# Moving the low halves of three weight tensors by 384 bytes in on-chip memory

## The chip, the cores and the metric

The kernel runs on one core of a Trainium2 chip. It is timed as one program: the metric is the device time of one execution in microseconds (us), and the number that stands for the kernel is the median of several executions. Beside the timed executions there is one that the hardware profiler recorded; all rows of views in this document come from such a recorded execution. Engines are named as the profile names them: PE is the matrix engine (TensorE), PEld its loading of weights, DVE is VectorE, ACT is ScalarE, POOL is GpSimd, SP is SyncE, which issues the DMAs.

## The reference

An attention layer with product features feeds a gated feed-forward layer with a mixing step along the sequence. Cut to what matters:

```python
# 4 batches, 4 heads, 1088 positions, head width 32; model width 128, hidden 1024
def phi(x):                                   # 8 x 8 products of two small projections
    a = np.einsum('rd,bhsd->bhsr', S1, x)
    b = np.einsum('rd,bhsd->bhsr', S2, x)
    return np.einsum('bhsi,bhsj->bhsij', a, b).reshape(*x.shape[:-1], 64)
kv  = np.einsum('bhsf,bhsd->bhfd', phi(k), v)
num = np.einsum('bhsf,bhfd->bhsd', phi(q), kv)
den = np.einsum('bhsf,bhf->bhs', phi(q), phi(k).sum(2))[..., None] + 1e-06
x   = (num / den) with heads joined           # 4 x 1088 x 128
h   = np.maximum(x @ w_in, 0.0)
u, v = h[..., :512], h[..., 512:]
v_n = (v - mean(v)) / sqrt(var(v) + 1e-06)    # over the 512 columns
v_s = np.einsum('ts,bsd->btd', w_spatial, v_n) + b_spatial[None, :, None]
out = (u * v_s) @ w_out
```

The step with `w_spatial` (1088 x 1088, applied to 512 columns of each of four batches) is most of the arithmetic.

## The kernel before

**Three products for one.** Every large matmul is split into a high and a low part of each operand, in a rounded four-byte format (float32r), and made of three matmuls: high by high, high by low, low by high. `mm3` (lines 424 to 427) does it for the dense layers. For the spatial step, `high` issues `vh` by `wTh` (line 943) and `vl` by `wTh` (line 945), and `low` issues `vh` by `wTl` (line 952); the last, half-filled block of 64 rows is done with the extra tile `v9` (line 954). In all of these the first-named operand, `vh` or `vl`, is the stationary one: PE loads it as 128 x 128 weights (a row LDWEIGHTS of PEld with the same line) while the matmul before still streams its own moving operand.

**Tiling.** A batch has 1088 output positions, cut into three column blocks of 424, 332 and 332 (`CH`), and 512 hidden columns, cut into four groups `d` of 128. One block (d, c) of the spatial step runs over nine steps `kt` along the contracted positions; each step is three matmuls in the order 943, 945, 952, and the last step is 943, 954. So a block streams 26 matmuls into one bank of PSUM (`sp`). Around the blocks stand the groups of three matmuls for `u` (tile `pu`, weights `wih0` and `wil0`, moving operand `x`), for the output layer (tile `po`, weights `woh` and `wol`, moving operand `g` or `x`), and for the next batch's attention and hidden layer (tile `sd`). The first batch is different: its first column block runs `kt` by `kt` over all four d as the data arrive, with lines 943 and 945 alone in turn, and the line 952 follows after it.

**Who writes the low parts.** `vl` is written by DVE (line 892 in the first batch, line 863 later), `wil0` and `wol` once at the start by DVE (line 435), each as the full value less its rounded high part. No DMA reads or writes them.

**What sets the order.** A planner in the kernel (`Order`) has a list of all operations with their costs and due times, orders them for all engines before the program is built, and the instructions are emitted in that order. Addresses play no part in it.

**Where tiles lie.** Most tiles of on-chip memory (SBUF) get their home when first used. The large weights have theirs at the head of `tile_kernel`, in a fixed sequence (lines 377 to 386), each right behind the one before in every partition. In the built program this gives, in bytes from the start of a partition and modulo 256:

| tiles | address | modulo 256 |
|---|---|---|
| `vh`, `wih0`, `woh` | 1632, 20064, 22112 | 96, 96, 96 |
| `ka1` (384 bytes) | 24160 | 96 |
| `vl`, `wil0`, `wol` | 24544, 40928, 42976 | 224, 224, 224 |
| `wT`, columns of block 0 / 1 / 2 | from 45088 | 32 / 240 / 240 |
| `x`, columns of block 0 / 1 / 2 | from 133408 | 32 / 192 / 240 |
| `g`, 424-wide / 332-wide pieces | from 128032 | 32 / 240 |
| `v9` (the last step's weights) | 158688 | 224 |

One step of `kt` is 2048 bytes in `vh` and `vl` and 4608 bytes in `wT`, one d is 512 bytes, so every weight that PE loads from a tile has the remainder that stands in the table.

Of the kernel before, what the change touches and what calls it, by code (L numbers as in the profile page):

```python
# [356 lines left out]
def tile_kernel(ctx: ExitStack, tc: tile.TileContext, kT, qT, vA, sks, idn, msk, wT, w_in, w_out, bsp, out):  # L357
# [12 lines left out]
    def weights(*names):  # L370
        for x in names:
            if x in ("vh", "vl"):
                homes[x] = const.tile([P, NS if x == "vh" else NK, ND, P], F32R, name=x)
            else:
                fixed[x] = const.tile([P, DH], F32R, name=x)

    homes["ka", 0] = const.tile([P, 96], F32, name="ka0")
    fixed["b32"], fixed["mask_sb"] = const.tile([P, 16], F32, name="b32"), const.tile([P, 6], F32, name="mask_sb")
    weights("vh", "wih0", "woh")
    homes["ka", 1] = const.tile([P, 96], F32, name="ka1")  # L380
    weights("vl", "wil0", "wol")
    homes["rec", 0] = const.tile([P, 3 * H], F32, name="rec0")
    homes["wT"] = const.tile([P, 2 * NS * PITCH], F32R, name="wT")
    homes["g"] = const.tile([P, SB_BUFS["g"], G_PITCH], F32R, name="g")
# [143 lines left out]
    wol = tl(None, "wol", [P, ND, DM], F32R)  # L528
# [583 lines left out]
```

## Time and profile before

| | |
|---|---|
| median of 3 executions | 331.39 us (331.07 to 331.58) |
| the profiled execution, its own time | 331.01 us |
| its span, first to last instruction | 329.2 us |
| PE busy | 323.0 us, 98% of the span, 2308 matmul records |
| PEld busy | 311.2 us, 95% |
| DVE, ACT, POOL busy | 200.3, 158.0, 59.4 us |
| granted PE clock | 1.0 throughout |

So 1.8 us of the profiled execution's time lie outside the span. A row of a timeline has the start and the length of an instruction; matmuls are pipelined, their lengths are modelled and overlap, so the pace of PE is read from the distance between two starts and not from the lengths. A row of groups has line, engine, operation, output and inputs, sizes, count, busy time and mean length of one.

### The profile page before, as it was taken

The page shows a single profiled execution, that of the slowest core. Times are in us where ns is not written, and L with a number is a line of the kernel's source. Part 1 is how long each engine was busy: PE and PEld are TensorE (multiplying, and loading weights), DVE is VectorE, ACT ScalarE, POOL GpSimd, SP SyncE. Part 2 cuts the span into 40 slices and gives each one's busy share as a digit, 9 for nine tenths or more (in the row PEclk, how much of TensorE's full clock was granted, in tenths as well). Part 3 has the DMA queues.
Part 4 walks back from the last instruction along what each step waited for, and adds up shares of the span by engine and source line. Part 5 has one row for each costly group of instructions (what it writes and reads, how often), then busy time and mean ns, then how long its engine had stood idle before and what let it go on. Part 6 is the DMA issues. An engine that isn't in the chain of part 4 may idle for free.

```text
span 329.2 us, 6032 instructions
## 1 busy us (share of the span) xinstructions
PE 323.0 (98%) x2308; PEld 311.2 (95%) x2308; DVE 200.3 (61%) x449; ACT 158.0 (48%) x365; POOL 59.4 (18%) x69
## 2 busy tenths in 40 slices
PE   8998999999999999999999999999999999999996
PEld 7987999999989899999999999999999999999995
DVE  4999995453799873769994277897722341221212
ACT  2589865444566651576553446564331252111122
POOL 1000216654114144411231225201000000000000
PEclk9999999999999999999999999999999999999999
DMA  6831449676111167500150353000000010000001
GB/s 218 304 94 51 122 136 277 153 131 161 60 47 44 20 127 147 148 2 24 47 96 1 77 111 60 2 0 0 3 0 2 0 47 23 0 2 1 0 2 68
DMA packets 18365, 23.10 MB, mean 70 GB/s; under 512 B 3104, under 2 KB 18080, under 8 KB 18336
## 3 DMA queue, kind: packets, MB, share of 16 engines
q1 hardware_dynamic: 18336, 22.71, 27.2%
q8 instruction: 18, 0.29, 0.4%
q14 instruction: 11, 0.09, 0.1%
HBM read 13.78 MB, written 2.23 MB: 49 GB/s over the span
## 4 chain that ended last, share of the span: by engine, by line
PE 76%; DVE 9%; ACT 5%; DMA 5%; SPq 2%; issue 1%; DVEq 0%; ACTq 0%
PE sp L943 18%; PE sp L945 16%; PE sp L952 16%; PE sd L425 3%; PE sd L426 3%; PE sd L427 3%; PE po L426 2%; DMA pl<-in_wT 2%; PE pu L425 2%; SPq L432 2%; DVE wT L554 2%; PE pu L427 2%; PE pu L426 2%; PE po L427 2%; PE po L425 2%; PE sd L638 2%
## 5 line engine op out<-in xcount | busy, mean ns | idle before, releaser
L943 PE MATMUL sp<-wT,vh 128*128 128x332 f32 (+1 forms) x414 | 134.4, 325 | 0.0
L945 PE MATMUL sp<-wT,vl 128*128 128x332 f32 (+1 forms) x368 | 119.1, 324 | 0.0
L952 PE MATMUL sp<-wT,vh 128*128 128x332 f32 (+1 forms) x368 | 116.9, 323 | 0.0
L943 PEld LDWEIGHTS sp<-wT,vh 128*128 128x128 f32 x414 | 77.9, 188 | 1.3
L945 PEld LDWEIGHTS sp<-wT,vl 128*128 128x128 f32 x368 | 69.2, 188 | 0.6
L952 PEld LDWEIGHTS sp<-wT,vh 128*128 128x128 f32 x368 | 69.1, 188 | 0.2
L979 DVE TENSOR_TENSOR u<-sp,u 128x332 f32<-128x332 f32 (+1 forms) x40 | 20.5, 514 | 38.3 <-PE sp L954 26.9
L435 DVE TENSOR_TENSOR g<-u,g 128x332 fp32r<-128x332 f32 (+1 forms) x38 | 21.7, 570 | 25.7 <-PE po L426 18.9
L504 ACT CAST g<-u 128x332 fp32r<-128x332 f32 (+1 forms) x38 | 17.9, 485 | 40.2 <-DVE u L979 25.8
L935 ACT ACTIVATE u<-pu 128x332 f32<-128x332 f32 (+1 forms) x40 | 18.5, 463 | 36.1 <-PE pu L427 35.1
L801 DVE BATCH_NORM_STATS2 st<-vt 128x6 f32<-128x512 f32 x36 | 24.2, 688 | 5.1 <-ACT vt L799 4.9
L779 DVE RECIPROCAL c<-c 128x384 f32<-128x384 f32 (+1 forms) x9 | 21.8, 2418 | 9.2 <-ACT c L777 9.2
L799 ACT ACTIVATE vt<-sd 128x512 f32<-128x512 f32 x36 | 21.4, 601 | 10.9 <-PE sd L427 10.3
L748 POOL TENSOR_TENSOR pl<-pl,pl 128x384 f32<-128x384 f32 (+1 forms) x18 | 19.0, 1059 | 33.6 <-DMA pl<-abT 33.4
L861 ACT CAST vh<-vt 128x384 fp32r<-128x384 f32 x36 | 17.4, 510 | 14.4 <-DVE vt L821 8.4
L438 POOL TENSOR_TENSOR r<-pl,r 128x384 fp32r<-128x384 f32 (+1 forms) x18 | 17.5, 982 | 37.1 <-ACT r L504 37.0
L863 DVE TENSOR_TENSOR vl<-vt,vh 128x384 fp32r<-128x384 f32 (+1 forms) x36 | 20.2, 578 | 2.8 <-ACT vh L861 2.7
L821 DVE TENSOR_SCALAR vt<-vt,mv,sm 128x512 f32<-128x512 f32 x32 | 17.4, 579 | 0.0
L438 POOL TENSOR_TENSOR r<-c,r 128x384 fp32r<-128x384 f32 (+1 forms) x9 | 9.7, 1082 | 40.0 <-ACT r L504 40.0
L425 PE MATMUL pu<-x,wih 128*128 128x332 f32 (+1 forms) x48 | 16.0, 334 | 0.8 <-ACT kp L935 0.8
L426 PE MATMUL pu<-x,wih 128*128 128x332 f32 (+1 forms) x48 | 15.7, 327 | 0.0
L427 PE MATMUL pu<-x,wil 128*128 128x332 f32 (+1 forms) x48 | 15.7, 327 | 0.0
(161 smaller groups left out, 522.2 us busy)
## 6 DMA issues: line engine op xcount, KB each, us to landing
pl<-in_wT SPq DMA_DIRECT2D x18, 166.0 KB, 2.3
v<-in_vA SPq DMA_DIRECT2D x12, 198.0 KB, 4.2
kt<-in_kT SPq DMA_DIRECT2D x12, 192.0 KB, 3.5
pl<-abT SPq DMA_DIRECT2D x12, 192.0 KB, 4.3
pl<-in_wT SPq DMA_DIRECT2D x9, 212.0 KB, 3.6
c<-in_qT SPq DMA_DIRECT2D x9, 192.0 KB, 3.5
pl<-abT SPq DMA_DIRECT2D x24, 72.0 KB, 3.4
out<-u SPq DMA_DIRECT2D x6, 166.0 KB, 1.8
```

What stands on the lines that cost most here:

```text
L425: nc.tensor.matmul(o, ah, bh, start=start, stop=False)
L426: nc.tensor.matmul(o, ah, bl, start=False, stop=False)
L427: nc.tensor.matmul(o, al, bh, start=False, stop=stop)
L435: return lambda: nc.vector.tensor_tensor(out=o(), in0=a(), in1=bb(), op=ALU.subtract)
L438: return lambda: nc.gpsimd.tensor_tensor(out=o(), in0=a(), in1=bb(), op=ALU.subtract)
L779: op("DVE", 135 + 6.3 * n, lambda x32=x32, n=n: nc.vector.reciprocal(out=x32[:, :n], in_=x32[:, :n]), w=[x32])
L799: op("ACT", c_act(512, True), lambda pv=pv, t=t: nc.scalar.activation(vt[:, t], pv.ap, AF.Relu), r=[pv], w=[(vt, t)])
L801: op("DVE", 690, lambda stats=stats, t=t: nc.vector.bn_stats(out=stats.ap, in_=vt[:, t]), r=[(vt, t)], w=[stats])
L943: nc.tensor.matmul(sp[:, :cw], vh[:, kt], wTh[:, kt, cs], start=(kt == 0), stop=False)
L945: nc.tensor.matmul(sp[:, :cw], vl[:, kt], wTh[:, kt, cs], start=False, stop=False)
L952: nc.tensor.matmul(sp[:, :cw], vh[:, kt], wTl[:, kt, cs], start=False, stop=False)
L979: op("DVE", c_dve(cw), lambda: nc.vector.tensor_tensor(out=u.ap, in0=sp[:, :cw], in1=u.ap, op=ALU.mult), r=[sp], w=[u], lead=LEAD[1])
```

## The change

The tile `ka1`, 384 bytes, changes places with the three low tiles in the fixed sequence: before, it lies between the high and the low tiles; now it lies behind the low ones.

```diff
--- before
+++ after
@@ -377,8 +377,8 @@
     homes["ka", 0] = const.tile([P, 96], F32, name="ka0")
     fixed["b32"], fixed["mask_sb"] = const.tile([P, 16], F32, name="b32"), const.tile([P, 6], F32, name="mask_sb")
     weights("vh", "wih0", "woh")
+    weights("vl", "wil0", "wol")
     homes["ka", 1] = const.tile([P, 96], F32, name="ka1")
-    weights("vl", "wil0", "wol")
     homes["rec", 0] = const.tile([P, 3 * H], F32, name="rec0")
     homes["wT"] = const.tile([P, 2 * NS * PITCH], F32R, name="wT")
     homes["g"] = const.tile([P, SB_BUFS["g"], G_PITCH], F32R, name="g")
```

In the built program `vl`, `wil0` and `wol` move from 24544, 40928 and 42976 to 24160, 40544 and 42592, that is from 224 to 96 modulo 256. The distance from `vh` to `vl` was 22912 bytes and is 22528. `ka1` moves from 24160 to 44640 and stays at 96 modulo 256. Every other tile stays at its address, and the instructions, their order on each engine and the semaphores that they wait for are the same.

## The prediction

> **What bounds the kernel now.** I read the page's totals and chain first, then PE's groups, then PE's timeline start by start.
>
> ```profile
> span 329.2 us, 6032 instructions
> PE 323.0 (98%) x2308; PEld 311.2 (95%) x2308; DVE 200.3 (61%) x449; ACT 158.0 (48%) x365; POOL 59.4 (18%) x69
> PEclk9999999999999999999999999999999999999999
> PE 76%; DVE 9%; ACT 5%; DMA 5%; SPq 2%; issue 1%; DVEq 0%; ACTq 0%
> ```
>
> PE is busy 98% of the span at the full granted clock, and 76% of the chain that ended last is PE. What is left to win on PE is its pace. The timeline of a late block, with nothing of DVE beside these rows, shows two paces on the same lines:
>
> ```profile
> 289.53 0.31 PE L943 MATMUL sp<-wT,vh 128*128 128x332 f32 x1
> 289.68 0.31 PE L945 MATMUL sp<-wT,vl 128*128 128x332 f32 x1
> 289.83 0.32 PE L952 MATMUL sp<-wT,vh 128*128 128x332 f32 x1
> ...
> 290.74 0.32 PE L952 MATMUL sp<-wT,vh 128*128 128x332 f32 x1
> 290.90 0.31 PE L943 MATMUL sp<-wT,vh 128*128 128x332 f32 x1
> 291.04 0.31 PE L945 MATMUL sp<-wT,vl 128*128 128x332 f32 x1
> ...
> 293.10 0.31 PE L943 MATMUL sp<-wT,vh 128*128 128x332 f32 x1
> ```
>
> From 289.53 to 290.90 there are nine matmuls in 1.37 us, 152 ns each; from 290.90 to 293.10 fifteen in 2.20 us, 146.7 ns each. I call the second pace even and the first slow. Both use 96 for `vh`, 224 for `vl` and 240 for `wT`, modulo 256, so the address of one matmul does not decide its pace; what went before does. The even pace includes lines 945, whose weights lie at 224: 290.90 to 291.04 is the interval in which such a weight is loaded. So a weight at 224 costs nothing by itself, and whatever the change can do lies in how often PE is slow. After 108 us, the stretch in which PE sets the end, the groups are:
>
> ```profile
> L943 PE MATMUL sp<-wT,vh 128*128 128x332 f32 x216 | 67.4, 312 | 0.0
> L952 PE MATMUL sp<-wT,vh 128*128 128x332 f32 x192 | 59.7, 311 | 0.0
> L945 PE MATMUL sp<-wT,vl 128*128 128x332 f32 x192 | 59.7, 311 | 0.0
> L943 PE MATMUL sp<-wT,vh 128*128 128x424 f32 x105 | 36.9, 352 | 0.0
> L945 PE MATMUL sp<-wT,vl 128*128 128x424 f32 x93 | 32.6, 351 | 0.0
> L952 PE MATMUL sp<-wT,vh 128*128 128x424 f32 x93 | 32.5, 350 | 0.0
> ```
>
> ```profile
> L952 PE MATMUL sp<-wT,vh x368: 309/312/358, 43.6 to 323.1; 128*128 128x332 f32 x130, 128*128 128x424 f32 x54
> L952 PE MATMUL po<-wT,vh x16: 348/348/357, 49.1 to 58.3; 128*128 128x424 f32 x16
> ```
>
> A length in these rows is the distance to the next start plus 162 ns (309 stands for 147, 348 for 186), so mean less smallest is the mean loss to slow pace: 3, 2, 2 ns at 332 columns and 4, 3, 2 ns at 424. Summed with the counts: 216 x 3 + 192 x 2 + 192 x 2 + 105 x 4 + 93 x 3 + 93 x 2 = 2.3 us. That bounds a gain from these lines.
>
> **The change part by part.** No instruction is added, removed or reordered, and no DMA touches the tiles; DVE's writes and PE's loads of three tiles get other addresses.
>
> *DVE's writes* I cost at nothing. The same operation on 512 elements writes `vl` at 224 and `vh` at 96 (line 901, half the partitions):
>
> ```profile
> L892 DVE TENSOR_TENSOR vl<-vt,vh x7: 661/679/684, 30.5 to 41.0; 128x512 fp32r<-128x512 f32 x7
> L901 DVE TENSOR_TENSOR vh<-vt,vh x1: 687/687/687, 42.2 to 42.2; 64x512 fp32r<-64x512 f32 x1
> ```
>
> The difference, 8 ns either way over 43 such writes, is 0.3 us of DVE, mostly beside PE.
>
> *PE's loads.* The question is which sequence of loads brings PE back to the even pace. I went through all starts after 62 us and looked at each slow matmul and the next of the same width. In a block the weights' remainders run 96 (943), 224 (945), 96 (952), 96 (943), and so on: two loads in a row with one remainder occur once per step, from 952 to the next 943. In that place the next interval is even in 29 of 67 cases at 332 columns and 17 of 22 at 424. In the other two places it is even in 7 of 177 (332) and 11 of 76 (424). First and last of the 67, with the 952 ahead of them:
>
> ```profile
> 64.23 0.31 PE L952 MATMUL sp<-wT,vh 128*128 128x332 f32 x1
> 64.38 0.31 PE L943 MATMUL sp<-wT,vh 128*128 128x332 f32 x1
> ...
> 320.86 0.32 PE L952 MATMUL sp<-wT,vh 128*128 128x332 f32 x1
> 321.02 0.31 PE L943 MATMUL sp<-wT,vh 128*128 128x332 f32 x1
> ```
>
> So PE recovers at step boundaries only. Two things happen there at once: the weights keep their remainder, and the moving operand goes from `wTl` back to `wTh`. The first batch separates them in part:
>
> ```profile
> 31.84 0.36 PE L943 MATMUL po<-wT,vh 128*128 128x424 f32 x1
> ...
> 43.24 0.35 PE L943 MATMUL po<-wT,vh 128*128 128x424 f32 x1
> 43.43 0.35 PE L943 MATMUL sp<-wT,vh 128*128 128x424 f32 x1
> 43.62 1.65 PE L952 MATMUL sp<-wT,vh 128*128 128x424 f32 x8
> 45.11 0.35 PE L954 MATMUL sp<-wT,v 66*128 66x424 f32 x1
> ```
>
> From 31.84 to 43.24, 943 and 945 alternate, so no two loads share a remainder: 58 matmuls in 11.40 us, 196.6 ns each, never even. From 43.43 to 45.11 all weights are `vh`: nine in 1.68 us, 186.7 ns, even at once. I therefore take the weights' remainder as the likelier cause. After the change all loads in a block but the last (`v9`) share 96, and each slow matmul would have the chance of 43% (332) or 77% (424) that now only the boundary has.
>
> *The sum.* After 108 us there are 43 slow stretches at 332 columns, 4.4 matmuls long on average (189 matmuls, 1.07 us above the even pace), and 41 at 424, 2.7 long (112 matmuls, 0.70 us). With chance p at every matmul a stretch that was L long becomes (1 - (1 - p)^L) / p: 1.9 and 1.2 on average. That saves 0.62 us and 0.38 us, 1.0 us together. For `pu` and `po`, whose third matmul gains a shared remainder, I take nothing: their second, which has one already (`wih0`, `woh` twice), recovers in only 10 of 72 cases.
>
> Before 108 us I count nothing, though PE would win 0.57 us in the first batch's alternation and 0.3 us from 62 to 108. PE stands there for DVE:
>
> ```profile
> 62.85 0.31 PE L425 MATMUL po<-g,woh 128*128 128x332 f32 x1
> 63.52 0.42 PE L426 MATMUL po<-g,woh 128*128 128x332 f32 x1 [0.35 <-DVE g L435]
> ...
> 107.06 0.31 PE L425 MATMUL po<-g,woh 128*128 128x332 f32 x1
> 107.92 0.41 PE L426 MATMUL po<-g,woh 128*128 128x332 f32 x1 [0.56 <-DVE g L435]
> ```
>
> The start at 107.92 is 0.86 us behind its forerunner and is released by DVE; the cover is DVE's queue ahead of `g`. An earlier PE only waits longer there. If DVE followed PE instead, the cover would be gone and up to 0.87 us would be added to the gain. The profiled execution goes from 331.01 to 330.0 us; it lies 0.38 us under the median of 331.39, so the median goes to 330.4.
>
> The Trainium skill speaks against any effect: "TensorE: Matmul & The Clock Gate", in the section on what each phase is for, gives PE two independent read ports and says that loading the next weights takes nothing from the running matmul, and "SBUF — State Buffer" states 16-byte lines, on which 96 and 224 both start. By these rules the sum is zero and the time 331.4. The trace agrees for the even pace and has nothing on why the slow one lasts.
>
> **The rivals.** *Nothing changes: 331.4 us.* Recovery at the boundary belongs to the moving operand or to PE's queue. For it: in `pu` and `po` two loads of one tile in a row rarely recover (10 of 72). Against it: the alternation at 31.84. That addresses matter at all, on the moving side, two groups with the same weights show: `pu` moving from 192 is never even (0 of 48), from 240 in 21 of 48.
>
> ```profile
> 139.58 0.31 PE L425 MATMUL pu<-x,wih 128*128 128x332 f32 x1
> 140.02 0.31 PE L943 MATMUL sp<-wT,vh 128*128 128x332 f32 x1
> ...
> 298.56 0.32 PE L425 MATMUL pu<-x,wih 128*128 128x332 f32 x1
> 299.02 0.31 PE L425 MATMUL po<-g,woh 128*128 128x332 f32 x1
> ```
>
> Three matmuls each: 0.44 us from 240, 0.46 us from 192.
>
> *Slower: the shared remainder holds PE in the slow pace.* A block at 96 throughout would drop out of the even pace at 945 as `pu` does from 192. Price: after 108 us all 600 matmuls at 332 columns would lose 5.5 ns (152.2 less 146.7) and all 291 at 424 about 9.9 (196.6 less 186.7), 6.2 us in place of 2.3: 335.3 us. It decides from the point where the slow share grows by a sixth (0.66 of 3.9 us). Against it: from 952 to 943, with equal remainders, an even PE never fell back (0 of 156).
>
> *The gain is eaten by DVE: 331.2 us.* If PE, early by 1 us, meets DVE's results late after 108 us as at 107, most of it turns into waiting. The six groups show no idle time of PE there, so this is small.
>
> That the tiles don't move is excluded by the addresses of the built program.
>
> **How the numbers follow.** Chances: recovery at every matmul 0.52, nothing 0.34, slower 0.10, eaten 0.04. The prediction is the first's, 330.4 us; its own range is 329.5 (the 0.87 us before 108 us come through too) to 330.9 (half the saving). The second case lies at 331.1 to 331.7, so a range of 329.5 to 331.8 leaves out most of the slower case and the tails. A change of 0.2% (0.66 us) is about what can be told from none. The first case is faster by more in 0.44 and within it in 0.08; the second gives 0.03, 0.28 and 0.03; the slower one 0.08 slower and 0.02 same; the eaten one 0.04 same. Faster 0.47, same 0.42, slower 0.11.
>
> **What would show it.** Right: from 31.84 on the alternation runs at about 187 ns instead of 196.6; slow stretches in blocks end at any of the three lines, with means of the six groups near 310 and 349; starts at 62.85 and 107.06 come earlier, those at 63.52 and 107.92 do not. Wrong: the alternation stays at 196.6 ns and stretches still end at step boundaries, which leaves the moving operand or the queue; or intervals of 945 near 152 ns become the rule.

## The result, and the profile after

The change made the kernel slower by 0.3%. Its median is 332.62 us (331.04 to 333.25, 17 executions) against 331.72 us (330.99 to 332.62, 17 executions) of the kernel before on the same chip: ratio 1.0029, 95% interval 1.0015 to 1.0043. The forecast was 330.4 us, with a range up to 331.8. The profiled execution took 332.81 us. Totals and chain of the changed kernel's page:

```profile
span 331.0 us, 6032 instructions
PE 324.7 (98%) x2308; PEld 313.1 (95%) x2308; DVE 200.7 (61%) x449; ACT 158.0 (48%) x365; POOL 59.2 (18%) x69
PEclk9999999999999999999999999999999999999999
PE 84%; DVE 8%; ACT 4%; DMA 1%; issue 1%; DVEq 0%
```

The clock is granted in full as before, DVE has 0.4 us more, PE 1.7 us. The groups after 108 us, as the prediction showed them of before:

```profile
L943 PE MATMUL sp<-wT,vh 128*128 128x332 f32 x216 | 67.7, 314 | 0.0
L945 PE MATMUL sp<-wT,vl 128*128 128x332 f32 x192 | 60.0, 312 | 0.0
L952 PE MATMUL sp<-wT,vh 128*128 128x332 f32 x192 | 59.9, 312 | 0.0
L943 PE MATMUL sp<-wT,vh 128*128 128x424 f32 x105 | 37.0, 352 | 0.0
L945 PE MATMUL sp<-wT,vl 128*128 128x424 f32 x94 | 33.0, 351 | 0.0
L952 PE MATMUL sp<-wT,vh 128*128 128x424 f32 x94 | 32.8, 349 | 0.0
```

At 424 columns the means are 352, 351 and 349, where they were 352, 351 and 350. At 332 columns each line lost 1 to 2 ns (they were 312, 311, 311). So the loss is in the narrow blocks, and PE still waits for nobody there. From start to start it is again a matter of two paces. A stretch of a late block:

```profile
306.29 0.31 PE L943 MATMUL sp<-wT,vh 128*128 128x332 f32 x1
306.44 0.31 PE L945 MATMUL sp<-wT,vl 128*128 128x332 f32 x1
306.59 0.31 PE L952 MATMUL sp<-wT,vh 128*128 128x332 f32 x1
306.75 0.32 PE L943 MATMUL sp<-wT,vh 128*128 128x332 f32 x1
...
307.66 0.31 PE L943 MATMUL sp<-wT,vh 128*128 128x332 f32 x1
...
308.11 0.35 PE L425 MATMUL po<-x,woh 128*128 128x424 f32 x1
```

From 306.29 to 308.11 twelve matmuls take 1.82 us, 152 ns each, past four step boundaries (306.29, 306.75, 307.20, 307.66). In the kernel before, the stretch at 289.53 was back at 146.7 ns after three steps.

I call a matmul of lines 943, 945 and 952 slow where the next start is more than 1.5 ns later than at the even pace (146.67 ns at 332 columns, 186.67 at 424). After 62 us the slow share at 332 columns went from 266 of 749 to 494 of 754, and the time above the even pace from 1.6 to 2.8 us. At 424 columns it stayed (114 and 113 of 297, 0.7 us). Aligned matmul by matmul, the trace after lags 0.72 us behind that of before at 66 us and 1.78 us at the last matmul: 1.06 us, for 1.2 us of slow pace. The lag before 62 us has other sources: 0.8 us arose within the first 10 us, ahead of all these matmuls; at 40 us it was down to 0.1 us, and a stop at 47 us, told below, brought it to 1.3 us before waits for DVE took part of it back. The medians lie 0.9 us apart, which fits the later part alone.

The first batch went as predicted in its pace, but nothing of it was left at its end:

```profile
32.69 0.35 PE L943 MATMUL po<-wT,vh 128*128 128x424 f32 x1
...
41.27 0.35 PE L943 MATMUL po<-wT,vh 128*128 128x424 f32 x1
...
46.53 0.53 PE L952 MATMUL sp<-wT,vh 128*128 128x424 f32 x2
47.88 0.39 PE L943 MATMUL sp<-wT,vh 128*128 128x332 f32 x1 [0.81 <-DVE kp L979]
```

From 32.69 to 41.27 46 matmuls of 943 and 945 take 8.58 us, 186.5 ns each; before it was 196.6 ns. At 47.88 PE has stood 0.81 us for DVE's line 979. In the kernel before, that place had no stop:

```profile
46.25 0.54 PE L952 MATMUL sp<-wT,vh 128*128 128x424 f32 x2
46.62 0.35 PE L943 MATMUL sp<-wT,vh 128*128 128x332 f32 x1
```

### The profile page after: what moved, and what is told of

It is laid out like the page before. It is cut to its first block, busy times and chain, and to the rows that moved or that the text cites. A ratio compares the mean times of both kernels' runs of the same rounds, so it can differ in the third digit from the quotient of the medians.

```text
span 331.0 us, 6032 instructions
## 1 busy us (share of the span) xinstructions
PE 324.7 (98%) x2308; PEld 313.1 (95%) x2308; DVE 200.7 (61%) x449; ACT 158.0 (48%) x365; POOL 59.2 (18%) x69
## 4 chain that ended last, share of the span: by engine, by line
PE 84%; DVE 8%; ACT 4%; DMA 1%; issue 1%; DVEq 0%
PE sp L943 19%; PE sp L952 17%; PE sp L945 16%; PE sd L425 3%; PE sd L427 3%; PE sd L426 3%; PE po L426 2%; PE po L425 2%; PE po L427 2%; PE pu L425 2%; PE pu L426 2%; PE pu L427 2%; PE sp L954 2%; PE sd L638 2%; PE sd L591 2%; DVE wT L554 2%
```

## The experiments

All of them change only where tiles lie, or where the second column block begins in `wT`; its width stays, and what is computed too. Two theories at the start: the **shared remainder** (recovery depends on two weights in a row having one remainder, the prediction's) and the **combination** (what counts is how moving operand and weights lie to each other). The table has all runs; its columns: vl's address less vh's, and that of the moving column blocks 0 / 1 / 2 less vh's, both modulo 256; slow share per block after 62 us in per cent; the time above the even pace that these matmuls lose there; and the ratio of times to the kernel before on the same chip. The shares of a layout come from one recorded execution, in which two blocks at one distance differ by up to 17 points (63 and 80% in wT_up96).

| kernel | vl - vh | wT - vh | slow, % | us | ratio (95%) |
|---|---|---|---|---|---|
| before | 128 | 192/144/144 | 38/34/37 | 2.3 | 1 |
| the change | 0 | 192/144/144 | 38/64/67 | 3.5 | 1.0029 (1.0015 to 1.0043) |
| vl_alone | 0 | 192/144/144 | 37/69/71 | 3.6 | 1.0037 (1.0019 to 1.0055) |
| dense_alone | 128 | 192/144/144 | 35/26/28 | 1.9 | 0.9987 (0.9972 to 1.0003) |
| swapped | 128 | 64/16/16 | 78/24/28 | 3.0 | 1.0017 (0.9999 to 1.0036) |
| all224 | 0 | 64/16/16 | 94/71/64 | 5.3 | 1.0102 (1.0080 to 1.0125) |
| low160 | 64 | 192/144/144 | 89/84/81 | 5.6 | 1.0132 (1.0114 to 1.0151) |
| low32 | 192 | 192/144/144 | 68/91/94 | 5.8 | 1.0119 (1.0100 to 1.0137) |
| after_c1at32 | 0 | 192/192/144 | 32/40/64 | 3.0 | 1.0025 (1.0011 to 1.0039) |
| before_c1at32 | 128 | 192/192/144 | 35/36/31 | 2.2 | 1.0010 (0.9995 to 1.0026) |
| dense_v9at96 | 128 | 192/144/144 | 37/30/29 | 2.1 | 0.9989 (0.9967 to 1.0010) |
| change_off512 | 0 | 192/144/144 | 37/70/64 | 3.5 | 1.0037 (1.0013 to 1.0061) |
| dense_c1at96 | 128 | 192/0/144 | 36/93/28 | 3.7 | 1.0051 (1.0031 to 1.0071) |
| dense_c1at160 | 128 | 192/64/144 | 35/62/30 | 2.8 | 1.0033 (1.0018 to 1.0048) |
| all_up64 | 128 | 192/144/144 | 36/28/29 | 2.0 | 0.9987 (0.9964 to 1.0009) |
| wT_up32 | 128 | 224/176/176 | 100/86/89 | 6.5 | 1.0171 (1.0116 to 1.0226) |
| wT_up96 | 128 | 32/240/240 | 100/63/80 | 5.3 | 1.0088 (1.0054 to 1.0122) |
| wT_up224 | 128 | 160/112/112 | 100/88/74 | 6.5 | 1.0129 (1.0101 to 1.0156) |

**The two halves of the change.** First `vl` alone, then the dense layers' low weights alone; `ka1` marks the step from 96 to 224.

```diff
-    weights("vh", "wih0", "woh")
+    weights("vh", "wih0", "woh", "vl")
     homes["ka", 1] = const.tile([P, 96], F32, name="ka1")
-    weights("vl", "wil0", "wol")
+    weights("wil0", "wol")
```

> Only vl at 96 modulo 256; wil0 and wol stay at 224. Theory of the shared remainder (high and low weights of a 332-wide block at one remainder hold PE slow): all of the change's loss, +0.7 to +1.1 us against the kernel before, mean lengths of the 332-wide lines 943, 945, 952 after 62 us of 315, 313, 312 as in the changed kernel, against 313, 311, 311 before; the first batch's alternation at 187 ns. Theory of the start (the loss is 0.8 us in the first DMAs and mere chance): within 0.3 us of before, whatever the pace.

For dense_alone, `"wil0", "wol"` stand in the first line and `"vl"` alone in the second.

> Only wil0 and wol at 96; vl stays at 224. Shared remainder in the spatial blocks: as before within 0.3 us, 332-wide means 313, 311, 311, the first batch's alternation at 196 ns. If the dense groups carry the loss: +0.5 us or more, and longer groups of lines 425 to 427.

`vl` alone has the whole loss (+0.37%), the dense weights none (-0.13%, an interval that just touches no change). The groups of dense_alone after 62 us, then those of vl_alone:

```profile
L943 PE MATMUL sp<-wT,vh 128*128 128x332 f32 x275 | 85.9, 313 | 0.0
L945 PE MATMUL sp<-wT,vl 128*128 128x332 f32 x244 | 75.8, 311 | 0.0
```

```profile
L943 PE MATMUL sp<-wT,vh 128*128 128x332 f32 x275 | 86.5, 315 | 0.0
L945 PE MATMUL sp<-wT,vl 128*128 128x332 f32 x244 | 76.3, 313 | 0.0
```

**Other remainders of the weights.** All at 224; high at 224 and low at 96; low at 160; low at 32:

```diff
--- before
+++ all224
-    weights("vh", "wih0", "woh")
    homes["ka", 1] = const.tile([P, 96], F32, name="ka1")
-    weights("vl", "wil0", "wol")
+    weights("vh", "wih0", "woh", "vl", "wil0", "wol")
--- before
+++ swapped
-    weights("vh", "wih0", "woh")
+    weights("vl", "wil0", "wol")
    homes["ka", 1] = const.tile([P, 96], F32, name="ka1")
-    weights("vl", "wil0", "wol")
+    weights("vh", "wih0", "woh")
```

In low160 `rec0` (64 bytes with its filling) stands between high and low weights and `ka1` behind them; in low32 both stand between:

```diff
--- before
+++ low160
     weights("vh", "wih0", "woh")
-    homes["ka", 1] = const.tile([P, 96], F32, name="ka1")
+    homes["rec", 0] = const.tile([P, 3 * H], F32, name="rec0")
     weights("vl", "wil0", "wol")
-    homes["rec", 0] = const.tile([P, 3 * H], F32, name="rec0")
+    homes["ka", 1] = const.tile([P, 96], F32, name="ka1")
--- before
+++ low32
     weights("vh", "wih0", "woh")
     homes["ka", 1] = const.tile([P, 96], F32, name="ka1")
+    homes["rec", 0] = const.tile([P, 3 * H], F32, name="rec0")
     weights("vl", "wil0", "wol")
-    homes["rec", 0] = const.tile([P, 3 * H], F32, name="rec0")
```

> All six weight tensors at 224 (ka1 put ahead of them; the low ones keep their addresses of before, the high ones move by 384 bytes). Shared remainder hurts at 332 columns: as slow as the change, +0.7 to +1.1 us, 332-wide means 315, 313, 312. Rival, the remainder 96 is what hurts beside a moving operand at 240: as fast as before or faster, 0 to -0.8 us, 332-wide means 312 or less. The first batch's alternation at 187 ns by the first, since the remainder is shared.

> Low tensors at 96, high ones at 224: two remainders 128 apart as before, exchanged. Shared remainder: as before within 0.3 us, alternation of the first batch at 196 ns. Rival, 96 for vl beside 240 hurts: +0.3 us or more with the interval of line 943 (in which vl is loaded) the long one; rival, 96 for any weight hurts: faster than before by up to 0.5 us, since only a third of the loads are at 96.

> Low tensors at 160, high ones at 96: 64 apart instead of 128 or 0 (rec0, not ka1, lies between them). If only an equal remainder hurts in the 332-wide blocks, they are as even as before (a quarter to a third of the matmuls slow, means 313, 311, 311) and the time is within 0.3 us of before. If it is the distance of 128 that helps, they are as slow as in the change: two thirds slow, means 315, 313, 312, +0.7 us or more.

> Low tensors at 32, high ones at 96: 192 apart. As with 160: only an equal remainder hurts, then as before within 0.3 us; the distance of 128 helps, then +0.7 us or more. A rival by the moving operand (a weight loaded at 32 beside a moving operand that starts at 32 collides): the 424-wide blocks get slower, means above 352, 351, 350.

Equal remainders are bad at 224 as at 96 in the narrow blocks (71 and 64%), so 96 is nothing special. In all224 two expectations failed: the loss is 3.4 us and not 0.7 to 1.1, with the wide block slow in 94%, and the first batch's alternation is not at 187 ns though all weights share a remainder (193.2 ns in the mean of 58 matmuls). Weights 64 or 192 apart are worse still. swapped settles the shared remainder: in its narrow blocks PE regains the even pace in 40 of 86 cases from 943 to 945, where the remainder goes from 224 to 96, and in 1 of 33 from 952 to 943, where it is the same. What it gains there it loses in the wide block, which moves from 32. Its groups after 62 us:

```profile
L952 PE MATMUL sp<-wT,vh 128*128 128x332 f32 x246 | 76.3, 310 | 0.0
L945 PE MATMUL sp<-wT,vl 128*128 128x332 f32 x245 | 76.0, 310 | 0.0
...
L945 PE MATMUL sp<-wT,vl 128*128 128x424 f32 x96 | 34.1, 355 | 0.0
L952 PE MATMUL sp<-wT,vh 128*128 128x424 f32 x96 | 34.0, 354 | 0.0
```

The narrow blocks have 310 where the kernel before has 311, the wide one 355 and 354 for its 351 and 350: one set of weights, and the two column blocks answer in opposite ways.

**Width or address of the moving operand?** The second column block begins 12 columns later in `wT`, so it moves from 32 as block 0 does, and stays 332 wide; once with the order of the change, once with that of before.

```diff
-AT = [0, 436, 820]
+AT = [0, 448, 820]
```

> The changed kernel with the columns of block 1 of wT at 32 modulo 256 instead of 240 (an offset of 448 columns for 436); block 2 stays at 240, widths as they are. If the moving operand's remainder takes part, block 1 recovers at any of the three lines as the 424-wide blocks at 32 do, and its slow share falls to about 40% while block 2 stays at two thirds: -0.3 to -0.6 us against the change. If only the weights' remainders count (or the width of 332), both blocks stay alike at two thirds and the time is that of the change within 0.3 us.

> The kernel before with the columns of block 1 of wT at 32 instead of 240. If the moving operand's remainder takes part, block 1 differs from block 2 in slow share by more than the 5 points by which blocks 1 and 2 may scatter; if not, both stay near a third and the time is within 0.3 us of before.

With equal remainders of the weights, block 1 goes from 64 to 40% slow, while block 2, which stayed at 240, has 64%. With weights 128 apart it stays (34 and 36%). So with equal remainders the address decides and not the width. The time barely follows: block 1's gain is 0.3 us of 3.5.

**The weights of the last step, and the size of the distance.** The four `v9` tiles moved to 96 as well; and the change with 512 bytes between high and low weights, since all layouts with equal remainders so far were 0 modulo 2048 apart.

```diff
--- dense_alone
+++ dense_v9at96
-    weights("vh", "wih0", "woh", "wil0", "wol")
+    weights("vh", "wih0", "woh", "wil0", "wol", "v90", "v91", "v92", "v93")
--- the change
+++ change_off512
-    weights("vh", "wih0", "woh")
-    weights("vl", "wil0", "wol")
+    weights("vh", "wih0", "woh", "sqh", "vl", "wil0", "wol", "sql")
```

(A tile whose name begins with v or s is 128 columns wide in `weights`.)

> Layout of dense_alone (low weights of the two dense layers at 96 modulo 256, vl at 224), with the four v9 tiles, the weights of the product at L954, moved from 224 to 96 as well; wT and what lies above it move up by 2048 bytes, so their remainders stay. If the product at L954 costs its 3 ns extra and knocks TensorE out of its even pace because its weight lies at 224: its interval falls to 147 ns at 332 columns and 187 at 424, fewer batches are slow, and the time is 0.3 to 0.8 us below dense_alone's. If that comes from its 66 rows, or from the vector engine's tile that it reads: the same as dense_alone within 0.3 us (331.2 to 331.8).

> The changed layout, with a 512-byte tile moved between the high and low recurrent weights: vl still lies at 96 modulo 256 as vh does, but the two are 23040 bytes apart, which is 512 modulo 1024 and modulo 2048, where they were 0 modulo 2048 in every layout with equal remainders so far. If the remainder modulo 256 is what counts: like the change, two thirds of the 332-column batches slow and 0.7 to 1.1 us over the kernel before. If it is the remainder modulo 1024 or 2048: about a third slow, and the time of the kernel before, within 0.4 us.

The interval of line 954 stays at 151 ns (332 columns) and 190 ns (424), and so do the slow shares: not the address of `v9` makes the block's end slow. change_off512 is as slow as the change: the remainder modulo 1024 or 2048 is not what counts. A step of 512 bytes can't tell a period of 256 from one of 512. The nearest to that is before_c1at32: its blocks 0 and 1 lie 192 bytes above `vh` modulo 256, but 448 and 192 modulo 512, and are 35 and 36% slow, though of different widths.

**Other places of the moving operand.** From dense_alone, the second column block begins 28 columns later in dense_c1at96 and 44 (480 for 464) in dense_c1at160.

```diff
-AT = [0, 436, 820]
+AT = [0, 464, 820]
```

> Layout of dense_alone, with the second column block of the moving operand wT beginning at 96 modulo 256 instead of 240 (by a column block that starts 28 columns later). If the moving operand's remainder has its own effect beside the weights': the slow share of block 1, 92 of 360 in dense_alone, becomes clearly another one (under 50 or over 160), and the time moves by 0.2 us or more. If not, it stays near a quarter to a third and the time within 0.3 us of dense_alone's, apart from some 0.1 us for the block's other width.

> As the run with 96, with the second column block of wT beginning at 160 modulo 256. If the pace goes by the distance between the remainders of moving operand and weights, 160 (64 from both 96 and 224) must be unlike 96 (equal to one of them): the slow share of block 1 then differs by a factor of two or more between the two runs. If the moving operand's remainder does not matter with weights 128 apart: both like dense_alone, 25 to 36 per cent slow.

At 96, with vh's own remainder, 335 of 360 matmuls of block 1 are slow; at 160, 224 of 363; blocks 0 and 2 stay. A block 1 of dense_c1at96:

```profile
200.26 0.32 PE L943 MATMUL sp<-wT,vh 128*128 128x332 f32 x1
...
203.79 0.31 PE L952 MATMUL sp<-wT,vh 128*128 128x332 f32 x1
203.94 0.32 PE L943 MATMUL sp<-wT,vh 128*128 128x332 f32 x1
```

Its 24 matmuls from 200.26 to 203.94 take 3.68 us, 153.3 ns each, though the weights are the good ones.

**Distance or absolute address?** From dense_alone, everything from `vh` up 64 bytes higher (`ka0` 64 bytes larger); then `wT` alone 32, 96 or 224 bytes higher, and what lies above it 256.

```diff
--- dense_alone
+++ all_up64
-    homes["ka", 0] = const.tile([P, 96], F32, name="ka0")
+    homes["ka", 0] = const.tile([P, 112], F32, name="ka0")
--- dense_alone
+++ wT_up32
-    homes["rec", 0] = const.tile([P, 3 * H], F32, name="rec0")
+    homes["rec", 0] = const.tile([P, 16 + 8], F32, name="rec0")[:, :3 * H]
     homes["wT"] = const.tile([P, 2 * NS * PITCH], F32R, name="wT")
+    pad = const.tile([P, 56], F32, name="pad")
```

For 96 and 224 bytes the 8 is 24 and 56, and `pad` has 40 and 8 columns.

> Layout of dense_alone with everything from the high weights up moved by 64 bytes: vh at 160 modulo 256, vl at 32, the column blocks of wT at 96, 48 and 48. All distances between tiles stay. Theory: only the distances modulo 256 between moving operand and weights set the pace. Then the slow shares are those of dense_alone (105 of 297, 92 of 360, 110 of 393) within 15 points, and the time is within 0.4 us of its. Rival: the absolute remainders count: then at least one block's share changes by 25 points or more and the time rises by 0.7 us or more.

> Layout of dense_alone with the moving operand wT alone 32 bytes up (what lies above it 256 bytes up, so at the same remainders): blocks at 64, 16 and 16, so 224, 176 and 176 bytes above vh's remainder. So far with weights 128 apart: distance 0 gave 93 per cent slow, 16: 24 to 26, 64: 62 to 78, 144: 26 to 35, 192: 36. If the distance sets the pace: blocks 1 and 2 (176) between 25 and 40 per cent, block 0 (224) unknown, between the 36 at 192 and the 93 at 0. If the moving operand's remainder plays no part of its own: all stay at 25 to 36.

> As wT_up32 with 96 bytes: blocks at 128, 80 and 80, so 32, 240 and 240 bytes above vh's remainder. If the distance sets the pace: block 0 (32) between the 25 at 16 and the 70 at 64; blocks 1 and 2 (240) near those of 224 in block 0 of wT_up32, and towards the 93 at 0. If it does not: 25 to 36 everywhere.

> As wT_up32 with 224 bytes: blocks at 0, 208 and 208, so 160, 112 and 112 bytes above vh's remainder. If the distance sets the pace: block 0 (160) as at 144 to 192, 25 to 38 per cent slow; blocks 1 and 2 (112) between the 70 at 64 and the 30 at 144. A share under 20 per cent in any block would be the first place where the even pace is nearly always regained, and would take 0.3 us or more off that block.

all_up64 keeps the distances, and all three slow shares and the time stay (106 of 297, 99 of 357, 116 of 394). With `wT` alone moved, all three blocks get slow. The groups of wT_up32 after 62 us (its lines are one higher):

```profile
L944 PE MATMUL sp<-wT,vh 128*128 128x332 f32 x280 | 88.6, 317 | 0.2 <-DVE u L980 0.2
L953 PE MATMUL sp<-wT,vh 128*128 128x332 f32 x248 | 78.0, 315 | 0.0
L946 PE MATMUL sp<-wT,vl 128*128 128x332 f32 x248 | 78.0, 314 | 0.0
L944 PE MATMUL sp<-wT,vh 128*128 128x424 f32 x108 | 38.6, 357 | 0.0
```

Lines 943 (here 944) have 317 and 357, where dense_alone has 313 and 352. (In this profile the clock was below full in one early slice, so I use its ratio, 1.0171, only as an order of size.) My expectation of 25 to 40% at distance 176 was wrong: 86 and 89%. So were those for 160 (25 to 38% expected, 100 found), for 32 (25 to 70, 100) and for 112 (30 to 70, 74 and 88). The distance sets the slow share in the blocks, but not smoothly. With weights 128 apart: 93% at 0, 24 to 28 at 16, 100 at 32, 62 to 78 at 64, 74 to 88 at 112, 26 to 37 at 144, 100 at 160, 86 to 89 at 176, 35 to 38 at 192, 100 at 224, 63 to 80 at 240. Of these, 32, 160 and 224 were tried at 424 columns only, 64 and 192 at both widths, the others at 332 only. Of the distances tried only 16, 144 and 192 are good, and the kernel before already had 192 and 144.

No layout is surely faster than before. Three have the distances of before and the dense layers' low weights at 96 (dense_alone, dense_v9at96, all_up64): 0.9987, 0.9989 and 0.9987, each with an interval that reaches just past 1, and 0.2 to 0.4 us less slow pace. Such a lead of some 0.4 us was not shown.

## Why the prediction was wrong, by its steps

**What bounds the kernel** was right: the pace of PE, whose two values stayed what they were (146.7 and about 152 ns). In the table the ratio follows the time lost to slow pace: 1.2 us more of it for the change and 0.96 us in time, 3.0 and 3.4 us for all224. The bound of 2.3 us, made of rounded means, was high: by the starts that the prediction's own sum uses, the blocks lost 1.07 and 0.70 us after 108 us, 1.8 us in all.

**DVE's writes at nothing** held: line 892 takes 675 ns in the mean after, 677 before, where 8 ns either way had been allowed. (One of the first batch's eight writes of `vl` is POOL's: 1.30 us before and after.)

**"I therefore take the weights' remainder as the likelier cause"** is the step that failed, and with it "each slow matmul would have the chance of 43%". That recovery sits where two loads share a remainder was true of one layout only. After the change PE regains the even pace at 332 columns in 26 of 127 cases from 952 to 943, 20% where it had been 43 (29 of 67), and in 7 of 330 in the two other places (7 of 177 before). The stretches grew from 4.1 to 6.3 matmuls, and from 65 to 79 in number. At 424 columns it went the forecast's way in part (22 of 84 in the other places, 11 of 76 before), while the boundary fell to 6 of 17, and the slow share stayed at 38%. So the term of the sum had the wrong sign: after 108 us, where it took 1.0 us off, the narrow blocks lose 2.0 us to the slow pace where they lost 1.1, the wide ones 0.7 us as before. Recovery at the boundary had two explanations in the prediction, equal weights and the moving operand's return to `wTh`; neither holds in all layouts: in swapped it sits between 943 and 945, where the weights change and the moving operand does not.

**The first batch** was taken as the separating evidence. Its alternation did become even, as the prediction said it would. But equal remainders do not decide there. In all224 it is slow with equal ones. In dense_v9at96 and all_up64 it starts even with weights 128 apart, as in the six layouts where it is slow throughout (196.2 to 196.7 ns). And one trace has both paces at the same addresses. In all_up64:

```profile
32.01 0.35 PE L943 MATMUL po<-wT,vh 128*128 128x424 f32 x1
...
40.98 0.35 PE L943 MATMUL po<-wT,vh 128*128 128x424 f32 x1
41.27 0.46 PE L945 MATMUL po<-wT,vl 128*128 128x424 f32 x1
41.57 0.35 PE L943 MATMUL po<-wT,vh 128*128 128x424 f32 x1
...
42.94 0.35 PE L945 MATMUL sp<-wT,vl 128*128 128x424 f32 x1
```

From 32.01 to 40.98 48 matmuls take 8.97 us, 186.9 ns each. The next two starts come 0.1 us late each, and from 41.57 to 42.94 seven matmuls take 1.37 us, 195.7 ns each. The addresses alone don't fix the pace there, so the alternation at 31.84 did not show what I read from it. What decides behind such a stop is open.

**The cover before 108 us** was not put to the test, since PE came to the places named no earlier but later: by 1.37 us at 62.85 and by 0.97 us at 107.06. DVE's waits there took up 0.5 and 0.1 us of it. What the first batch's alternation gained, 0.4 us by 40 us, was followed by the stop of 0.81 us at 47.88, but the gain did not cause the stop. DVE's line 979 came 1.3 us later than before: 0.5 us was lag that it had already, and the line 554 ahead of it took 1.33 us in place of 0.49:

```profile
45.90 1.33 DVE L554 TENSOR_TENSOR wT<-pl,wT 128x332 fp32r<-128x332 f32 x1
47.15 0.58 DVE L979 TENSOR_TENSOR kp<-sp,kp 128x424 f32<-128x424 f32 x1
```

```profile
45.43 0.49 DVE L554 TENSOR_TENSOR wT<-pl,wT 128x332 fp32r<-128x332 f32 x1
45.85 0.59 DVE L979 TENSOR_TENSOR kp<-sp,kp 128x424 f32<-128x424 f32 x1
```

(The changed kernel first, then the one before.) The instruction of line 554 takes 1.31 to 1.33 us in 14 of the 18 recorded executions and 0.49 to 0.50 in the others, beside the same instruction of POOL each time. dense_alone has it too, and a stop of 0.63 us, though its alternation is as slow as before:

```profile
47.34 0.39 PE L943 MATMUL sp<-wT,vh 128*128 128x332 f32 x1 [0.63 <-DVE kp L979]
```

Why it takes the one time or the other was not shown.

**The rival on the slower side** came true with another cause and a smaller price. Its price, 335.3 us, had all matmuls slow; two thirds of the narrow ones were. Its argument, that the even pace would be lost in a block, is not what happened: after the change an even PE falls back in 0 of 58, 2 of 78 and 4 of 80 cases in the three places. It just regains the pace less often. The evidence held against it (no fall from 952 to 943) was true and said nothing on that. Its chance of 0.10 was too low: `pu`, never even when moving from 192, stood in the trace as a sign that the moving operand's address counts too, and I used it only to say that addresses matter.

The Trainium skill's rule in "TensorE: Matmul & The Clock Gate", in the section on what each phase is for, by which loading the next weights takes no read bandwidth from the running matmul, would by itself have given no change in any of these layouts. The runs don't agree with that forecast: with the same instructions the time moved by 0.96 us for the change and by 1.0% in all224. The measurement decides. Whether it is reading that the two disturb each other in was not shown.

## What to carry to other kernels

Where a kernel runs one matmul after the other, compare the start-to-start intervals of one shape: two values on one line mean that time lies in the pace, which no busy share shows. Then move the operands' start addresses as a thing to be measured, moving operand and weights together, modulo 256 bytes; here that cost up to about 1.3%, and no layout was surely faster than the one before. A correlation inside one layout (recovery where remainders are equal) is no cause until a second layout has kept it.

## What was not expected of the hardware

- How often a 128x128 matmul of this type runs at its slow pace depends on the distance modulo 256 bytes between moving operand and weights. With the same instructions and weights 128 apart, 35 to 38% of the intervals at 424 columns are slow at a distance of 192 and 100% at 224; at 332 columns 26 to 37% at 144 and 86 to 89% at 176. Everything 64 bytes higher, with the distances kept, changed no block's share by more than 2.2 points; another shift of everything was not tried, and the first batch's alternation did change by it, from slow to even.
- Adding 128 to the distance gave like values at 16 and 144 (24 to 28, 26 to 37), at 32 and 160 (100, 100) and at 112 and 240 (74 to 88, 63 to 80), but not at 64 and 192 (62 to 78, 35 to 38). I have no rule for it. Which resource is shared was not shown: the traces have the interval and nothing inside it.
- The slow pace is a state: once slow, PE stays so over many matmuls whose addresses run at the even pace elsewhere on the same lines (stretches of 6.3 matmuls in the mean at 332 columns after the change; in all_up64 186.9 ns in one alternation up to a stop and 195.7 ns behind it).
